# Reading rearranged columns back one slot later, and a second tile for the modulation's weights

## The chip, the cores and the metric

The kernel runs on one core of one Trainium2 chip. The metric is the device time of one execution in microseconds; the time of a kernel is the median over several executions.

## The reference

One row of 4096 tokens with 640 features goes through two networks, each behind a layer norm that is scaled and shifted by a modulation computed from `c`:

```python
mod = (_silu(c) @ w_mod).reshape(c.shape[0], 6, 1, -1)
sa, ca, ga, sb, cb, gb = (mod[:, 0], mod[:, 1], mod[:, 2], mod[:, 3], mod[:, 4], mod[:, 5])
h = _layernorm(x, axis=-1) * (1 + ca) + sa
x = x + ga * _A_ref(h, A_w1, A_b1, A_w2, A_b2)
h = _layernorm(x, axis=-1) * (1 + cb) + sb
x = x + gb * _B_ref(h, B_w_gate, B_w_up, B_w_down)
```

`_A_ref` is the first network: a real Fourier transform along the tokens, a two-layer complex MLP on each frequency (4 blocks of 160 features, relu between the layers, soft shrinkage with 0.01 behind them), and the inverse transform. `_B_ref` is the second network: `(silu(x @ w_gate) * (x @ w_up)) @ w_down` with 1728 hidden features. All data is float32.

## The kernel before

Matmuls run on float32r operands, each float32 operand split into a high and a low part, so that most products are three matmuls. The program has three stretches: layer norm and the first step of the Fourier transform; the first network's loop; the second network. The change lies in the loop.

The loop runs over 32 slots `p`, four to each of 8 chunks of frequencies (`ch = p // 4`, `b = p % 4`). Every engine executes its instructions in the order written here, and so does the queue of SP, which issues nearly all DMAs (`nc.sync.dma_start`): a DMA that waits holds all that is written behind it. In one slot PE does the following, in this order:

- `stage_l1` (lines 636 and 649): the first MLP layer of block `b`, from the chunk's tiles `z` (features 0 to 127 of a block) and `rz` (the narrow columns, features 128 to 159 of every block). Its third output goes to a PSUM bank that line 654 (`u`, on DVE, behind line 653 on ACT) evacuates.
- `stage_b` (line 552): the second Fourier step of the next chunk, from `g` and `tb`; twice where `b == 1`, once of them for the narrow columns.
- `stage_l2` (line 682): the second layer of the slot before, its results added into `tt` by DVE.
- `stage_i` (lines 735 to 737): the inverse step of a chunk seven slots back, in two halves, into `co`, which POOL's queue stores.

The narrow columns of the next chunk come out of `stage_b` in an order that `stage_l1` cannot use. They are rearranged through DRAM: `rem_high` (ACT, line 602) and `rem_low` (DVE, line 606) fill `rt`; `rem_move` stores `rt` into `rzd` (line 615) and reads it back in four DMAs into `rz` (line 618). All three are called in the slot with `b == 1`; `rz` is used first in the next slot with `b == 0`. Tile `rz` has two buffers.

The modulation is summed beside this: `mod_load(m, k)` loads 128 rows of one of its parts, 128 x 640, into `wm` (line 488, SP), and `mod_add(m, k)` (lines 493 and 495, DVE) multiplies it by a column of `sc` and adds it to `acc`. There are 20 such steps, five for each of four parts, and the tile `wm` has one buffer. The slots are written down in two tables, `mods` and `sums`; the list for a slot is called at the slot's end. For part `i` step `k`, the load is in slot 4 + 6i + k and the add in slot 5 + 6i + k, where it is followed by the load of the next step. So a load waits for the add written directly ahead of it, and has until the end of the next slot to land.

Other DMAs on SP in the loop: `move_x` in slots with `b == 0` (line 698, eight moves of `tt` into `xx`), `load_g` and `load_tb` in slots with `b == 3`, `load_e` in slot 26, and the loads of rows for the second network's start (`load_first_rows`, line 798) in slots 24 and 27 and behind the loop. Each slot's DMAs are issued in this order: `rem_move`, `move_x`, `load_g`, the slot's `mods`, `load_first_rows`.

The memory for a tile comes from pools. `low_p` holds `rt` and a tile `spare` that nothing uses; `p2` holds `wm`, `acc`, `xx` and others.

Of the kernel before, what the change touches and what calls it, by code (L numbers as in the profile page):

```python
# [6 lines left out]
F32 = mybir.dt.float32  # L7
# [6 lines left out]
P = 128  # L14
D = 640
# [6 lines left out]
NCH = 8  # L22
# [149 lines left out]
def body(tc, x, w1, b1, w2, b2, wg, wu, wd, c, wm, k_fa, k_tb, k_tx, k_bm, k_bx, k_ga, k_ge, k_id, out, dbg=None):  # L172
# [4 lines left out]
    def f32(ap):  # L177
        return ap.bitcast(F32)
# [21 lines left out]
    from contextlib import ExitStack  # L200
    with ExitStack() as top:
        low_p = top.enter_context(tc.tile_pool(name="low_p", bufs=1, reuse_waits="tile"))
        low_p.tile([P, 2552], F32, name="spare")
        per = top.enter_context(tc.tile_pool(name="per", bufs=1))
        ps = top.enter_context(tc.tile_pool(name="ps", bufs=2, space=PSUM))

# [30 lines left out]
        with ExitStack() as af:  # L237
# [47 lines left out]
            def weights_low(w, h, l, v, sg):  # L285
                dve.scalar_tensor_tensor(w[:, :, l], v, sg, f32(w[:, :, h]), op0=OP.mult, op1=OP.subtract)
# [182 lines left out]
            p2 = af.enter_context(tc.tile_pool(name="p2", bufs=1, side="right", reuse_waits="tile"))  # L469
# [14 lines left out]
            wmts = {}  # L484

            def mod_load(m, k):
                wmts[m, k] = p2.tile([P, D], F32, tag="wm", bufs=1, name=f"wm{m}_{k}")
                nc.sync.dma_start(wmts[m, k], wm[:, m, k, :])

            def mod_add(m, k):  # L490
# [37 lines left out]
            mods = {26: [(load_e,)]}  # L528
            sums = {}
            for i, m in enumerate((0, 2, 3, 4)):  # L530
                for k in range(5):
                    mods.setdefault(4 + 6 * i + k, []).append((mod_load, m, k))
                    mods.setdefault(5 + 6 * i + k, []).append((mod_add, m, k))
                sums.setdefault(11 + 6 * i if m < 4 else LAST, []).append((mod_sum, m, 1))
                if m == 2:
                    sums.setdefault(10 + 6 * i, []).append((mod_sum, m, 0))
# [7 lines left out]
            def width(ch):  # L544
                return 258 if ch == CE else 256

            def stage_b(ch, t):
                g, tb = gs[ch], tbs[ch]
                pb = bank0(1 if t == 4 else 0, [P, 2, 256], f"pb{ch}_{t}")
                col = slice(128 * t, 128 * t + 128)  # L550
                for j in range(4):
                    mm(pb[:, :, 64 * j:64 * j + 64], g[:, j, col], tb[:, j, :], start=True, stop=True)
                pbs[ch, t] = pb

            def evac_b(ch, t):
                pb = pbs[ch, t]
                z = lp.tile([P, 2, 2, 258], F32R, tag="z", bufs=4, name=f"z{ch}_{t}")
                zs[ch, t] = z
                act.activation(z[:, 0, :, 0:256], pb, AF.Identity, scale=ca1[:, t:t + 1])
                dve.scalar_tensor_tensor(z[:, 1, :, 0:256], pb, ca1[:, t:t + 1],  # L560
                                         f32(z[:, 0, :, 0:256]), op0=OP.mult, op1=OP.subtract)
                if ch == CE:
                    pool.tensor_copy(z[:, 0, :, 0:257:256], f32(edge[:, 0, t]))
                    pool.tensor_copy(z[:, 1, :, 0:257:256], f32(edge[:, 1, t]))
                    pool.tensor_copy(z[:, :, :, 257], zero[:, 0, 0])
# [8 lines left out]
            def evac_rh(ch, b):  # L574
                pb = pbs[ch, 4]
                if b == 0:
                    rzs[ch] = hp.tile([P, NB, 258], F32R, tag="rz", bufs=2, name=f"rz{ch}")
                    if ch == CE:
                        pool.tensor_copy(rzs[ch][:, :, 257], zero.rearrange("p a b c d -> p (a b c d)")[:, 0:4])
                q = slice(32 * b, 32 * b + 32)  # L580
                for i in range(2):
                    act.activation(rzs[ch][32 * i:32 * i + 32, b, 0:256], pb[q, i, :], AF.Identity,
                                   scale=ca1[q, 4:5])

            def evac_rl(ch, b):
                pb = pbs[ch, 4]
                r = rzs[ch]
                q = slice(32 * b, 32 * b + 32)
                for i in range(2):
                    rh = slice(32 * i, 32 * i + 32)  # L590
                    rl = slice(64 + 32 * i, 96 + 32 * i)
                    dve.scalar_tensor_tensor(r[rl, b, 0:256], pb[q, i, :], ca1[q, 4:5],
                                             f32(r[rh, b, 0:256]), op0=OP.mult, op1=OP.subtract)
                    if ch == CE:
                        pool.tensor_copy(r[rh, b, 0:257:256], f32(edge[q, 0, 4, i]))
                        pool.tensor_copy(r[rl, b, 0:257:256], f32(edge[q, 1, 4, i]))
# [3 lines left out]
            def rem_high(ch):  # L600
                rt = rts[ch] = low_p.tile([P, 2, 2, 258], F32R, tag="rt", name=f"rt{ch}")
                act.activation(rt[:, 0, :, 0:256], pbs[ch, 4], AF.Identity, scale=ca1[:, 4:5])

            def rem_low(ch):
                rt = rts[ch]
                dve.scalar_tensor_tensor(rt[:, 1, :, 0:256], pbs[ch, 4], ca1[:, 4:5], f32(rt[:, 0, :, 0:256]),
                                         op0=OP.mult, op1=OP.subtract)
                if ch == CE:
                    for hl in range(2):
                        pool.tensor_copy(rt[:, hl, :, 0:257:256], f32(edge[:, hl, 4]))  # L610
                    pool.tensor_copy(rt[:, :, :, 257], zero[:, 0, 0])

            def rem_move(ch):
                NN = width(ch)
                nc.sync.dma_start(rzd[ch, :, :, 0:NN], f32(rts[ch].rearrange("p l i k -> p (l i) k")[:, :, 0:NN]))
                r = rzs[ch] = hp.tile([P, NB, 258], F32R, tag="rz", bufs=2, name=f"rz{ch}")
                for q in range(4):
                    nc.sync.dma_start(f32(r[32 * q:32 * q + 32, :, 0:NN]),
                                      rzd[ch].rearrange("(b e) q k -> q e b k", b=NB)[q, :, :, 0:NN])
# [183 lines left out]
            for p in range(LAST + 1):  # L803
                ch, b = p // 4, p % 4
                on(shrink, p - 6)
                on(stage_l1, p)

                if b == 0:
                    todo = [(ch, 3)]
                else:  # L810
                    todo = [(ch + 1, 4)] * (b == 1) + [(ch + 1, b - 1)]
                todo = [q for q in todo if q[0] < NCH]
                for q in todo:
                    stage_b(*q)
                    if q[1] < 4:
                        evac_b(*q)
                for f, *a in sums.get(p, ()):
                    f(*a)

                if p == 0:  # L820
                    evac_rh(0, 3)
                if b == 1 and ch + 1 < NCH:
                    rem_high(ch + 1)
                on(tail_l1, p)
                on(shrink_high, p - 6)
                if p == 0:
                    evac_rl(0, 3)
                if b == 1 and ch + 1 < NCH:
                    rem_low(ch + 1)
                    rem_move(ch + 1)  # L830
                on(stage_l2, p - 1)
                on(stage_i, p - 7)
                on(shrink_low, p - 6)
                if p < LAST:
                    on(shrink_parts, p - 5)
                if b == 0 and ch:
                    for i in range(4):
                        move_x(ch - 1, i)
                if p == 0:
                    for job in prep2[3:]:  # L840
                        weights_low(*job)
                if b == 3 and 2 < ch + 2 < NCH:
                    load_g(ch + 2)
                    load_tb(ch + 2)
                for f, *a in mods.get(p, ()):
                    f(*a)
                if p == LAST - 4:
                    cf += [rp.tile([P, 2, D], F32, tag=tag, name=f"cf{tag}") for tag in ("rm", "rr")]
                    load_first_rows(rb + 16, rl, nc.sync)
                elif p == LAST - 1:  # L850
                    load_first_rows(0, rb - 16, nc.sync)
# [107 lines left out]
        with ExitStack() as ff:  # L959
# [15 lines left out]
            for n, (k, p) in enumerate(WG):  # L975
                STG.append(("w", n))
                if k == "g" and p:
# [22 lines left out]
            bufs = {"R": 2, "h1": 1, "wb": 2, "wt": 2, "wd": 1, "wdh": 2, "wdl": 2, "pc": 4, "px": 2, "gt": 2, "ho": 2,  # L1000
                    "h32": 1, "sg": 4, "s": 5, "gx": 2, "rb0": 1, "rb1": 1, "ra0": 1, "ra1": 1}
# [1008 lines left out]
            mv, rs, _ = fst[3]  # L2010
# [25 lines left out]
            for t in range(NS):  # L2036
                for n in range(NW):
                    if sum_at(n) == t:
                        a, b = sum_w(n)
# [69 lines left out]
```

## Time and profile before

| | us |
|---|---|
| median of 3 runs | 1487.83 |
| lowest and highest | 1484.5, 1488.16 |
| the profiled execution | 1483.82 |
| its span | 1482.0 |
| loop of the first network, from about 60 to 312 of the span | 252 |
| second network, 312 to the end | 1170 |

The profile is that of one execution; its times are microseconds from the start of the span. A row of the timeline has the start, the duration, the engine, the line, what is written and read and how many instructions are merged in the row; in brackets stands the idle time ahead of it and what ended that. SPq is the queue of SP. The granted clock is that of the tensor engine as a share of full speed. The ends of pipelined matmuls are modelled, so spacings are taken from their starts.

### The profile page before, as it was taken

The numbers are of one execution on the slowest core, as the hardware profiler recorded it, in microseconds if no ns is written. First come the engines' busy times: TensorE is split into PE (matmuls) and PEld (weight loads), VectorE is DVE, ScalarE is ACT, GpSimd is POOL, SyncE is SP. The second block draws the span as 40 slices with busy tenths as digits, with TensorE's granted clock in tenths as the row PEclk, the third lists the DMA queues.
The fourth block names the chain that finished last, engine by engine and source line by source line (L and its number), as shares of the span: only waits on it lengthen the run. The fifth ranks groups of instructions, "written<-read, shape, count | busy, mean of one in ns | idle before, by whom it ended". The sixth has DMA issues, their size and how long they took to land.

```text
span 1482.0 us, 23780 instructions
## 1 busy us (share of the span) xinstructions
PE 1432.4 (97%) x8736; PEld 1356.8 (92%) x8736; DVE 1023.8 (69%) x1841; ACT 759.9 (51%) x1470; POOL 411.6 (28%) x528
## 2 busy tenths in 40 slices
PE   6999999898999999999999999999999999999999
PEld 2799999876888888899999999999999999999999
DVE  8567777678787787757877756878656555465653
ACT  7657888645444555445545535554443334344331
POOL 5400100034563443313433323433211121111111
PEclk9999999999999999999999999999999999999999
DMA  9966767738767977696677797566774345944422
GB/s 378 328 207 197 230 206 226 218 95 280 272 228 251 363 258 242 213 398 229 208 235 242 263 350 255 200 233 228 291 287 151 120 156 179 349 154 139 146 75 83
DMA packets 162405, 339.41 MB, mean 229 GB/s; under 512 B 20656, under 2 KB 85872, under 8 KB 160240
## 3 DMA queue, kind: packets, MB, share of 16 engines
q1 hardware_dynamic: 153776, 320.35, 63.5%
q0 software_dynamic: 6928, 14.91, 3.3%
q10 hardware_dynamic: 1584, 2.62, 0.5%
q8 instruction: 69, 1.13, 0.3%
q14 instruction: 48, 0.39, 0.1%
HBM read 238.35 MB, written 90.31 MB: 222 GB/s over the span
## 4 chain that ended last, share of the span: by engine, by line
PE 68%; DMA 10%; issue 10%; DVE 6%; POOL 3%; ACT 3%; SPq 1%; POOLq 0%; DVEq 0%; ACTq 0%
PE pd L1984 21%; PE pw L1790 7%; PE pw L1792 7%; PE pw L1791 7%; DMA wt<-td 4%; PE pg L1713 3%; PE pg L1714 3%; PE pg L1715 3%; PE pw L1801 2%; PE pw L1803 2%; PE pw L1802 2%; PE pc L682 2%; PE pl L636 2%; PE py L1443 2%; DMA hs<-ho 1%
## 5 line engine op out<-in xcount | busy, mean ns | idle before, releaser
L1984 PE MATMUL pd<-wdh,a 128*128 128x320 f32 x1672 | 382.4, 310 | 2.8 <-DVE a L1750 2.0
L1984 PEld LDWEIGHTS pd<-wdh,a 128*128 128x128 f32 x1672 | 282.9, 188 | 4.0 <-DVE a L1750 2.6
L1984 PE MATMUL pd<-wdl,a 128*128 128x320 f32 x868 | 267.3, 309 | 0.0
L1956 DVE TENSOR_TENSOR x<-x,pd 128x320 f32<-128x320 f32 x384 | 178.9, 482 | 100.7 <-PE pd L1984 93.2
L1246 DVE TENSOR_TENSOR wb<-r,wb 128x512 fp32r<-128x512 f32 (+3 forms) x172 | 162.8, 954 | 18.8 <-ACT wb L1243 17.4
L1984 PEld LDWEIGHTS pd<-wdl,a 128*128 128x128 f32 x868 | 163.1, 188 | 0.4
L1790 PE MATMUL pw<-h,wt 128*128 128x384 f32 x416 | 141.0, 339 | 6.4 <-DMA wt<-td 5.0
L1792 PE MATMUL pw<-h,wt 128*128 128x384 f32 x416 | 139.2, 335 | 0.0
L1791 PE MATMUL pw<-h,wt 128*128 128x384 f32 x416 | 139.2, 335 | 0.0
L1337 ACT ACTIVATE wdh<-wdr 128x640 fp32r<-128x640 f32 x84 | 60.6, 734 | 152.4 <-PE pd L1984 144.1
L1243 ACT ACTIVATE wb<-r 128x512 fp32r<-128x512 f32 (+3 forms) x172 | 117.9, 704 | 29.4 <-PE pw L1803 21.0
L1834 POOL TENSOR_TENSOR sg<-s_x,sg 128x384 f32<-128x384 f32 x24 | 25.1, 1048 | 351.7 <-DVE s_x L1816 351.7
L1792 PE MATMUL pw<-h,wb 128*128 128x384 f32 x312 | 104.7, 336 | 0.7 <-DVE wb L1246 0.7
L1790 PE MATMUL pw<-h,wb 128*128 128x384 f32 x312 | 105.0, 337 | 0.0
L1791 PE MATMUL pw<-h,wb 128*128 128x384 f32 x312 | 104.7, 335 | 0.0
L1715 PE MATMUL pg<-ht,wb 128*128 128x512 f32 x260 | 101.7, 391 | 2.2 <-DVE wb L1246 2.2
L1713 PE MATMUL pg<-ht,wb 128*128 128x512 f32 x260 | 102.3, 393 | 1.2 <-ACT wb L1243 1.2
L1714 PE MATMUL pg<-ht,wb 128*128 128x512 f32 x260 | 101.5, 390 | 0.0
L1341 DVE TENSOR_TENSOR wdl<-wdr,wdh 128x640 fp32r<-128x640 f32 x84 | 75.7, 910 | 33.6 <-ACT wdh L1337 33.4
L1837 DVE TENSOR_TENSOR a<-sg,a 128x384 fp32r<-128x384 f32 x104 | 71.9, 700 | 31.7 <-ACT a L1836 31.2
L1790 PEld LDWEIGHTS pw<-h,wt 128*128 128x128 f32 x416 | 78.1, 188 | 9.9 <-DMA wt<-td 4.1
L1791 PEld LDWEIGHTS pw<-h,wt 128*128 128x128 f32 x416 | 78.2, 188 | 0.0
(264 smaller groups left out, 3315.6 us busy)
## 6 DMA issues: line engine op xcount, KB each, us to landing
wt<-td SPq DMA_DIRECT2D x104, 512.0 KB, 5.2
hs<-ho SPq DMA_DIRECT2D x52, 512.0 KB, 5.4
h<-hs SPq DMA_DIRECT2D x32, 768.0 KB, 8.0
r<-in_B_w_gate_dram SPq DMA_DIRECT2D x36, 640.0 KB, 4.4
r<-in_B_w_up_dram SPq DMA_DIRECT2D x36, 640.0 KB, 4.8
wdr<-wdd SPq DMA_DIRECT2D x35, 640.0 KB, 4.5
td<-wt SPq DMA_DIRECT2D x25, 512.0 KB, 4.9
g<-s SPq DMA_DIRECT2D x28, 320.0 KB, 5.5
```

The lines of the kernel that those rows point to most:

```text
L1243: act.activation(wbs[t, n][:, 0, ks, e], raw[t, n][:, ks, e], AF.Copy)
L1246: dve.tensor_tensor(wbs[t, n][:, 1, ks, e], raw[t, n][:, ks, e], f32(wbs[t, n][:, 0, ks, e]), op=OP.subtract)
L1341: dve.tensor_tensor(l[:, f], wdraw[t, p][:, f], f32(h[:, f]), op=OP.subtract)
L1713: mm(b, wh, hh, start=(kk == 0), stop=False)
L1714: mm(b, wh, hl, start=False, stop=False)
L1715: mm(b, wl, hh, start=False, stop=(kk == 4))
L1790: mm(b, w(0, kp), a[:, kp, 0], start=start and kp == 0, stop=False, skip_group_check=not start)
L1791: mm(b, w(0, kp), a[:, kp, 1], start=False, stop=False, skip_group_check=not start)
L1792: mm(b, w(1, kp), a[:, kp, 0], start=False, stop=kp == 1, skip_group_check=not start)
L1837: Step("V", cv_ + 0.1, lambda: dve.tensor_tensor(o[:, 1], sg, f32(o[:, 0]), op=OP.subtract), (("ah", key),), ("act", t, fc, a), free=("sg" ...
L1956: dve.tensor_tensor(x2[:, e], x2[:, e], x[0][:, :320], op=OP.add)
L1984: mm(pd[g, hf][0][:, :320], l, m, start=i == 0, stop=i == len(s) - 1 and not (last and len(gs) > 1))
```

## The change

`rem_move` is cut in two: it keeps the store to `rzd`, and the allocation of `rz` and the four reads become `rem_read`, called in the slot with `b == 2`, ahead of that slot's `mods`. The tile of a modulation load is taken in turn from `p2` and from `low_p`, each with one buffer, so that there are two; `spare` shrinks by the 640 elements that the second takes. Every load stands one slot earlier in the table (3 + 6i + k), its add where it was.

```diff
-        low_p.tile([P, 2552], F32, name="spare")
+        low_p.tile([P, 1912], F32, name="spare")
...
             def mod_load(m, k):
-                wmts[m, k] = p2.tile([P, D], F32, tag="wm", bufs=1, name=f"wm{m}_{k}")
+                wmts[m, k] = (p2, low_p)[len(wmts) % 2].tile([P, D], F32, tag="wm", bufs=1, name=f"wm{m}_{k}")
                 nc.sync.dma_start(wmts[m, k], wm[:, m, k, :])
...
                 for k in range(5):
-                    mods.setdefault(4 + 6 * i + k, []).append((mod_load, m, k))
+                    mods.setdefault(3 + 6 * i + k, []).append((mod_load, m, k))
                     mods.setdefault(5 + 6 * i + k, []).append((mod_add, m, k))
...
             def rem_move(ch):
                 NN = width(ch)
                 nc.sync.dma_start(rzd[ch, :, :, 0:NN], f32(rts[ch].rearrange("p l i k -> p (l i) k")[:, :, 0:NN]))
+
+            def rem_read(ch):
+                NN = width(ch)
                 r = rzs[ch] = hp.tile([P, NB, 258], F32R, tag="rz", bufs=2, name=f"rz{ch}")
                 for q in range(4):
                     nc.sync.dma_start(f32(r[32 * q:32 * q + 32, :, 0:NN]),
...
                 if b == 1 and ch + 1 < NCH:
                     rem_low(ch + 1)
                     rem_move(ch + 1)
+                if b == 2 and ch + 1 < NCH:
+                    rem_read(ch + 1)
                 on(stage_l2, p - 1)
```

## The prediction

> **What bounds the kernel now.** I read the page first, then the busy time of each engine in the three stretches of the program, then the waits of the first network's stretch, and then its timeline on SP, DVE and PE.
>
> ```profile
> span 1482.0 us, 23780 instructions
> ...
> PE 1432.4 (97%) x8736; PEld 1356.8 (92%) x8736; DVE 1023.8 (69%) x1841; ACT 759.9 (51%) x1470; POOL 411.6 (28%) x528
> ...
> 60.00:312.00 252.00, 238.98 (x1810) 235.23 (x1809) 182.69 (x342) 179.48 (x374) 26.54 (x51) 0.98 0.68 211
> 312.00:1482.00 1170.00, 1145.56 (x6761) 1096.48 (x6759) 795.60 (x1363) 536.72 (x1023) 355.95 (x410) 1.00 0.66 226
> ```
>
> The two window rows give stretch and length, then busy time of PE, PEld, DVE, ACT and POOL, the granted clock, the DMA share and GB/s. PE bounds the whole program. The change touches only the stretch from 60 to 312, the slotted loop of the first network: there PE is busy for 239 of 252 us, at a mean clock of 0.98 instead of 1.00. Some 13 us of idle time and a little clock are all that can be won there. The waits say which idle time the change can reach.
>
> ```profile
> SPq L618 <- DMA rzd<-rt: 31.6, 7, 7.0
> ...
> DVE acc L495 <- DMA wm<-in_w_mod_dram: 13.5, 5, 6.7
> ...
> PE pi L735 <- DVE u L654: 6.8, 2, 4.9
> ```
>
> Read from the top: who waited for whom, us in total, times, longest. SP's queue stands seven times, once for each rearranged chunk, until the narrow columns have landed in DRAM (rzd); only then may line 618 read them back. DVE stands five times for a weight tile wm of the modulation. PE stands twice for `u`, an evacuation that DVE makes. The timeline shows that these are one chain; first SP's queue (start, duration, line, transfer, count):
>
> ```profile
> 110.70 0.57 SPq L615 DMA_DIRECT2D rzd<-rt  x1
> 114.89 1.74 SPq L618 DMA_DIRECT2D rz<-rzd  x4
> 116.74 5.83 SPq L488 DMA_DIRECT2D wm<-in_w_mod_dram  x2
> ...
> 255.47 0.54 SPq L488 DMA_DIRECT2D wm<-in_w_mod_dram  x1
> ...
> 257.62 0.59 SPq L615 DMA_DIRECT2D rzd<-rt  x1
> 265.29 1.79 SPq L618 DMA_DIRECT2D rz<-rzd  x4
> 267.18 0.38 SPq L488 DMA_DIRECT2D wm<-in_w_mod_dram  x1
> ```
>
> The wm loads at 116.74 and 267.18 are those of slots 5 and 25 (b = 1). They were free to go earlier, but they stand in the queue behind the four reads of rz, and those behind the landing of rzd. DVE and ACT at the same two places:
>
> ```profile
> 112.21 0.55 DVE L493 TENSOR_SCALAR acc<-wm,sc 128x640 f32<-128x640 f32 x1 [0.34 <-DMA wm<-in_w_mod_dram]
> ...
> 116.50 0.81 DVE L724 TENSOR_TENSOR xl<-xx,xh 128x640 fp32r<-128x640 f32 x1
> ...
> 118.70 0.38 ACT L653 ACTIVATE u<-pl 64x256 f32<-64x256 f32 x1
> ...
> 121.31 0.88 DVE L495 SCALAR_TENSOR_TENSOR acc<-wm,sc,acc 128x640 f32<-128x640 f32 x1 [3.99 <-DMA wm<-in_w_mod_dram]
> ...
> 123.51 0.47 DVE L654 SCALAR_TENSOR_TENSOR u<-pl,b1r,u 64x256 f32<-64x256 f32 x1
> ...
> 259.61 0.89 DVE L495 SCALAR_TENSOR_TENSOR acc<-wm,sc,acc 128x640 f32<-128x640 f32 x1 [0.19 <-DMA wm<-in_w_mod_dram]
> ...
> 264.24 0.82 DVE L724 TENSOR_TENSOR xl<-xx,xh 128x640 fp32r<-128x640 f32 x1
> ...
> 267.07 0.38 ACT L653 ACTIVATE u<-pl 64x256 f32<-64x256 f32 x1
> ...
> 271.74 0.89 DVE L495 SCALAR_TENSOR_TENSOR acc<-wm,sc,acc 128x640 f32<-128x640 f32 x1 [6.68 <-DMA wm<-in_w_mod_dram]
> ```
>
> The adds of slots 6 and 26 stand 3.99 and 6.68 us for those loads; the other three of the five waits are 13.5 - 10.7 = 2.8 us together. DVE works in order, so the evacuation of `u` (line 654) stands behind each add, and PE needs the PSUM bank that `u` frees. PE at both places and, between them, at a place where nothing waits:
>
> ```profile
> 121.79 0.30 PE L737 MATMUL pi<-xh,bm 128*128 128x320 f32 x1
> ...
> 124.04 0.49 PE L735 MATMUL pi<-xh,bm 128*128 128x320 f32 x1 [1.95 <-DVE u L654]
> ...
> 127.77 0.40 PE L636 MATMUL pl<-rz,w1c 128*128 128x256 f32 x2
> ...
> 262.67 0.31 PE L737 MATMUL pi<-xh,bm 128*128 128x320 f32 x1
> ...
> 263.96 0.40 PE L636 MATMUL pl<-rz,w1c 128*128 128x256 f32 x2
> ...
> 264.91 0.40 PE L636 MATMUL pl<-rz,w1c 128*128 128x256 f32 x2
> ...
> 269.30 0.30 PE L737 MATMUL pi<-xh,bm 128*128 128x320 f32 x1
> ...
> 274.46 0.64 PE L735 MATMUL pi<-xh,bm 128*128 128x320 f32 x1 [4.87 <-DVE u L654]
> ...
> 278.17 0.40 PE L636 MATMUL pl<-rz,w1c 128*128 128x256 f32 x2
> ```
>
> **The change, part by part.** *What the two stalls cost.* From the last matmul of line 737 ahead of the gap to the second rz run of line 636 behind it, the same work takes 264.91 - 262.67 = 2.24 us undisturbed, 127.77 - 121.79 = 5.98 us at the first stall and 278.17 - 269.30 = 8.87 us at the second. The excess is 3.74 + 6.63 = 10.37 us. Of it 1.95 + 4.87 = 6.82 us are gaps; the rest, 1.79 and 1.76 us, is slow work after the gaps:
>
> ```profile
> 117.00:128.00 11.00, 9.05 (x58) 8.80 (x57) 6.95 (x13) 6.70 (x15) 0.62 (x1) 0.84 0.61 177
> ```
>
> The granted clock around the first stall is 0.84, so even a gap of 1.95 us cost clock. Beside this row stands a rule of the Trainium skill, "TensorE: Matmul & The Clock Gate", section "HAM oscillation": only idle gaps of more than about 3.4 us re-throttle the clock. By that rule the first stall would be worth its gap alone, and the sum 10.37 - 1.79 = 8.58 us. Here the trace disagrees with it, and I take the measured 10.37.
>
> *Do both stalls go?* The add of slot 6 takes its tile from a load in slot 4 instead of 5, the add of slot 26 from slot 24 instead of 25; neither has a read-back ahead of it any more. The load that goes out at 255.47, in slot 24 behind the moves of the tt columns, has landed by 259.61 (the add there waited 0.19 us for it); in the changed kernel that place holds the tile of slot 26, which DVE wants at 264.24 + 0.82 = 265.06, so 5 us are spare. At 112.21 the tile of slot 4's place has landed likewise, and it is wanted at 116.50 + 0.81 = 117.31.
>
> *What is late next?* From add to `u` DVE needs 123.51 - 121.31 = 2.20 us. Started at 117.31, `u` begins at 119.51 (ACT's part of it is done at 118.70 + 0.38 = 119.08) and ends at 119.98; PE wants the bank at about 121.79 + 0.15 = 121.94, the spacing of these matmuls being about half of the 0.30 that one lasts. At the second place ACT is done at 267.45, `u` at 267.92, and PE wants it at 269.45. Margins 2.0 and 1.5 us: PE runs on.
>
> *The read-back, one slot later.* On SP its four DMAs move past the wm load of slot b = 1 and nothing else; POOL's queue is not touched. It still waits for the landing of rzd, which decided before. The load that now precedes it, in slot 5, waits for the add at 112.21, which ends at 112.76, 2.1 us ahead of 114.89; in slot 25 for the add at 259.61, which ends at 260.50, 4.8 us ahead of 265.29. So the read-back leaves when it left before. What it needs:
>
> ```profile
> L618 SPq DMA_DIRECT2D rz<-rzd x28: 309/424/1514, 94.0 to 266.6; - x28
> ...
> DMA to landing us min/median/max: 2.5/2.8/3.7
> ...
> 116.45 0.40 PE L636 MATMUL pl<-rz,w1c 128*128 128x256 f32 x2
> ...
> 257.36 0.40 PE L636 MATMUL pl<-rz,w1c 128*128 128x256 f32 x2
> ```
>
> One slot is 263.96 - 257.36 = 6.60 us of PE. Without the second stall PE asks for the last chunk's rz at 263.96 + 6.60 = 270.56; the last read starts at 266.6 and lands 2.8 to 3.7 us later, at 269.4 to 270.3. That margin is 0.3 to 1.2 us, the tightest of the change: the stall that goes was also cover for this read. Chunk 2, read at 114.89, asks at 116.45 + 6.60 = 123.05 and has it by 114.89 + 1.74 + 3.7 = 120.3: 2.7 us. Against the last chunk speaks a rule of the Trainium skill, "DMA: Bandwidth & Descriptors", section "Queues, rings and completion order": on each DMA engine descriptors are consumed in ring order, so the wm load that now stands ahead is served before the read. No run here shows that order yet.
>
> *Costs at nothing.* 28 reads and 20 loads stay 28 and 20, no compute instruction is added, and the second tile lies in memory that was spare. A load still waits in its slot for an add of the same slot, as before, so what stands behind it on SP (rzd, load_g, the tt moves) is held no longer than now. Two slots are 13.2 us for a transfer for which this took at most:
>
> ```profile
> L488 SPq DMA_DIRECT2D wm<-in_w_mod_dram x20: 328/365/1392, 108.7 to 272.6; - x20
> ...
> DMA to landing us min/median/max: 3.0/4.2/5.7
> ```
>
> *Does the gain reach the end?* In the chain that ended last, at the seam of the two networks, stands the load of the first network's last rows, which the next matmuls wait for:
>
> ```profile
> 311.99 2.95 DMA cfrr<-s
> ```
>
> It follows the last store of the first network, the loads of the second stand behind it on SP, and all of them move up together. The second network is PE at 1145.56 of 1170 us and is unchanged; I take its change as 0, with 3 us to either side, since the three runs of this kernel spread over 3.7 us (1484.5 to 1488.16).
>
> The sum: 10.37 us less at most 0.4 for a read that is just late, 10.2 taken. The profiled execution took 1483.82 us (span 1482.0), so it would be 1473.6. The median of the runs is 4.0 us above the profiled one; the same 10.2 from 1487.83 give 1477.6.
>
> **The rivals.** *The read-back becomes the late one.* If the wm load of slot 25 does delay it, by up to the 1.5 us that lie between landings of 4.2 and 5.7, the last chunk starts about 1.2 us late, and after such a gap the slow clock takes up to 1.8 more: 10.4 - 3 = 7.4 us gained, 1480.4. For it speaks the margin of 0.3 us; against it that the load has 4.8 us of lead and lands in 4.2.
>
> *The second network gives it back.* Its own waits for DMAs could swallow the lead; nothing says so, since it depends on the first in a chain, but should 7 us or more of the 10.2 go, the time is 1484.6 to 1487.8, no change.
>
> *The change does not do what it says.* An add still waits, say because the load two slots ahead is held by the tt moves on SP. One of two stalls left gives 1481.2 (the first gone alone, 1484.1).
>
> *Slower.* The load in slot b = 1 waits for an add and holds the read-back behind it in every chunk; PE then starts each chunk late. Place: the first rz matmul of chunks 2 to 7. It decides once the add ends later than rzd lands (2.1 us of margin in slot 5, 4.8 in slot 25) and by more than the read's own margin (2.7 in chunk 2). To end 4.5 us above the present time it must cost 10.4 + 4.5 = 14.9 us, 2.5 in each of six chunks: the add of slot 5 would have to end 7.3 us later than it does (2.1 + 2.7 + 2.5), while the change takes waits out of DVE. With it the time is about 1493.
>
> **How the numbers follow.** About 0.3% of the time, 4.5 us, is what a measurement of this kernel can tell from no change. Forecast as summed 0.72; read-back late 0.11; one stall left 0.06, half of it still faster by 0.3%; given back 0.07; slower 0.04. That makes faster 0.86, same 0.10, slower 0.04. The range runs from 1477.6 less 3 for the second network and 2 for the runs' level, 1472.6, up to the late read with 3 us given back, 1483.4.
>
> **What would show it.** Right: in the changed profile the adds of line 495 no longer wait longer than 1 us, the wm load of slot 25 stands ahead of the rz reads on SP, the two gaps of line 735 are gone, the mean clock of the stretch is above 0.98, and the stretch is 10 us shorter. Wrong: a new gap ahead of the rz matmuls of line 636 at the start of the last chunk, an add that still waits, or a length from the loop's end to the span's end that has grown instead.

## The result, and the profile after

| | before | after |
|---|---|---|
| median of 5 runs, us | 1485.26 | 1475.6 |
| lowest to highest, us | 1484.5 to 1488.16 | 1473.78 to 1480.82 |
| profiled execution (span), us | 1483.82 (1482.0) | 1477.1 (1475.3) |

The ratio of after to before is 0.9934, with a 95% interval of 0.9911 to 0.9957: 9.7 us less by the medians, 6.4 to 13.2 us by the interval. In a second comparison (the run named e10 below, six runs) it is 0.9951, 0.9938 to 0.9964, or 7.3 us. The change makes the kernel faster, by 0.5 to 0.7%.

The page of after, and then its busy time in the two stretches, from the windows view (columns as in the prediction; the boundary is moved by 7 us):

```profile
span 1475.3 us, 23779 instructions
...
PE 1431.8 (97%) x8736; PEld 1358.4 (92%) x8736; DVE 1026.0 (70%) x1841; ACT 759.5 (51%) x1470; POOL 409.8 (28%) x528
```

```profile
60.00:305.00 245.00, 237.91 (x1813) 233.99 (x1812) 184.66 (x344) 179.23 (x375) 26.46 (x52) 0.99 0.71 218
305.00:1475.00 1170.00, 1146.24 (x6758) 1099.33 (x6758) 795.78 (x1361) 536.57 (x1022) 354.68 (x410) 1.00 0.66 226
```

That the second stretch keeps its 1170 us follows from where I put the boundary. Counted by the work, from the first matmul of slot 0 to the first of `first_y`, the step behind the loop, there are 233.3 us instead of 241.4, 8.1 less. From there to the end are 1170.4 us instead of 1169.5, and slot 0 starts 0.4 us later; together these are the 6.7 us of the span. The clock of the loop's stretch rose from 0.98 to 0.99. SP's queue, DVE and PE at the two places (timeline of after; from line 616 on its lines stand three to five further down: 618 is 621, 636 is 639, 737 is 740):

```profile
110.83 0.57 SPq L615 DMA_DIRECT2D rzd<-rt  x1
112.47 0.33 SPq L488 DMA_DIRECT2D wm<-in_w_mod_dram  x1
115.24 1.75 SPq L621 DMA_DIRECT2D rz<-rzd  x4
118.12 0.35 SPq L488 DMA_DIRECT2D wm<-in_w_mod_dram  x1
...
253.63 0.59 SPq L615 DMA_DIRECT2D rzd<-rt  x1
256.77 0.34 SPq L488 DMA_DIRECT2D wm<-in_w_mod_dram  x1
261.53 1.78 SPq L621 DMA_DIRECT2D rz<-rzd  x4
263.41 1.32 SPq L522 DMA_DIRECT2D et<-in_k_ge_dram  x1
```

The wm load of slots 5 and 25 now goes out between the store of rzd and the read of rz, in time that SP spent waiting. Grouped by line, the adds of the loop:

```profile
L495 DVE SCALAR_TENSOR_TENSOR acc<-wm,sc,acc 128x640 f32<-128x640 f32 x16 | 14.0, 877 | 0.0
```

The last number is DVE's idle time ahead of them: 0.0, where it was 13.5 us. And PE at both places:

```profile
121.92 0.30 PE L740 MATMUL pi<-xh,bm 128*128 128x320 f32 x1
122.06 0.31 PE L738 MATMUL pi<-xh,bm 128*128 128x320 f32 x1
...
124.16 0.39 PE L639 MATMUL pl<-rz,w1c 128*128 128x256 f32 x2
...
265.66 0.30 PE L740 MATMUL pi<-xh,bm 128*128 128x320 f32 x1
...
267.90 0.40 PE L639 MATMUL pl<-rz,w1c 128*128 128x256 f32 x2
```

From 121.92 to 124.16 are 2.24 us, the undisturbed figure of the prediction, where there were 5.98. From 265.66 to 267.90 are 2.24 us as well, where there were 8.87.

### The profile page after: what moved, and what is told of

Same layout as the page of the kernel before. It is cut to its first block, busy times and chain, and to the rows that moved or that the text cites. A ratio compares the mean times of both kernels' runs of the same rounds, so it can differ in the third digit from the quotient of the medians.

```text
span 1475.3 us, 23779 instructions
## 1 busy us (share of the span) xinstructions
PE 1431.8 (97%) x8736; PEld 1358.4 (92%) x8736; DVE 1026.0 (70%) x1841; ACT 759.5 (51%) x1470; POOL 409.8 (28%) x528
## 4 chain that ended last, share of the span: by engine, by line
PE 50%; DMA 3%; DVE 1%; ACT 1%; issue 0%; POOL 0%; SPq 0%
PE pd L1989 19%; PE pw L1795 7%; PE pw L1797 7%; PE pw L1796 7%; DMA wt<-td 3%; PE pw L1806 2%; PE pw L1808 2%; PE pw L1807 2%; PE pr L1909 1%; PE py L1448 1%; PE pt L1512 1%; PE pd L1999 0%; DVE wdl L1346 0%; DVE ho L1553 0%; ACT h L1516 0%
```

## The experiments

Each is compared with the kernel before on the same chip. For the loop I give the length of slots 7 and 8 and of slots 27 and 28 in the profile of each run, counted from the first matmul of `stage_l1` of a slot to that of the next; the two stalls of before lie in them.

| run | slots 7 + 8 | slots 27 + 28 | all four | ratio to before, 95% interval |
|---|---|---|---|---|
| before | 16.97 | 22.40 | 39.37 | |
| after | 13.21 | 15.77 | 28.98 | 0.9934, 0.9911 to 0.9957 |
| e1, read-back alone | 13.22 | 22.97 | 36.19 | 0.9978, 0.9964 to 0.9993 |
| e2, tiles and early loads alone | 13.22 | 15.76 | 28.98 | 0.9935, 0.9915 to 0.9956 |
| e6, e1 with late load_e | 13.22 | 15.80 | 29.02 | 0.9933, 0.9909 to 0.9957 |
| e8, second tile alone | 15.67 | 22.71 | 38.38 | 0.9995, 0.9981 to 1.0009 |
| e5, after with read-back at b = 3 | 14.55 | 22.32 | 36.87 | 0.9971, 0.9956 to 0.9987 |
| e3, after with a third tt | 13.21 | 16.15 | 29.36 | 0.9936, 0.9913 to 0.9959 |
| e7, after with chunk 1 direct | 13.22 | 15.90 | 29.12 | 0.9930, 0.9904 to 0.9955 |
| e9, e3 and e7 | 13.22 | 15.86 | 29.08 | 0.9925, 0.9906 to 0.9945 |
| e10, after again | 13.22 | 16.64 | 29.86 | 0.9951, 0.9938 to 0.9964 |
| e4, before with adds on POOL | 13.22 | 28.24 | 41.46 | 1.0112, 1.0088 to 1.0136 |

**e1: the read-back move alone.** Before, with `rem_move` cut in two; tiles and loads as before.

```diff
+                if b == 2 and ch + 1 < NCH:
+                    rem_read(ch + 1)
```

> Only the read-back moves to the slot with b = 2; one wm tile, loads where they were. Theory A (what stalls PE is the wm load standing behind the read-back on SP): the load of slot 5 goes out when the add of its slot ends, at about 112.8, lands 3.0 to 5.7 us later, at 115.8 to 118.5, and is wanted at 117.3; the add waits at most 1.2 us, less than the 2 us that PE can spare. Both gaps of line 735 go, the loop is 10.4 us shorter than before, the time about 9 to 10 us less: as much as the whole change. Theory B (the second tile and the extra slot are what counts; the load still starts only after the add ahead of it): the waits shrink but stay over 2 us at one of the two places, and the gain is under 5 us.

Measured 1484.09 against 1486.23 us. Slots 7, 8 and 27 are as theory A has them (6.63, 6.59 and 6.63 us): both gaps of line 735 are gone. But the gain is that of theory B, because a third add became late (timeline of e1, SP, then DVE and PE):

```profile
260.88 1.98 SPq L621 DMA_DIRECT2D rz<-rzd  x4
262.96 1.67 SPq L522 DMA_DIRECT2D et<-in_k_ge_dram  x1
264.74 0.37 SPq L488 DMA_DIRECT2D wm<-in_w_mod_dram  x1
...
272.31 0.88 DVE L495 SCALAR_TENSOR_TENSOR acc<-wm,sc,acc 128x640 f32<-128x640 f32 x1 [5.24 <-DMA wm<-in_w_mod_dram]
...
273.34 2.27 PE L510 MATMUL pm<-ones,acc 128*128 128x1 f32 x10 [4.00 <-DVE acc L495]
```

The last wm load, of slot 26, now stands behind the read-back and behind `load_e` (1280 KB). In the kernel before, the stall of slot 27 had hidden that. The wait moved from the add of slot 26 to that of slot 27. The DMA engines served the load last as well: the packets of `load_e` start between 265.28 and 269.65, those of the wm load, issued 1.8 us behind it, between 269.13 and 270.97, and it lands 7.5 us after its issue (at most 5.7 in the kernel before).

**e2: the tiles and the early loads alone.** After, with the read-back in its old place.

```diff
                     rem_move(ch + 1)
-                if b == 2 and ch + 1 < NCH:
                     rem_read(ch + 1)
```

> Only the second wm tile and the loads one slot earlier; the read-back stays in the slot with b = 1, ahead of that slot's load. Theory A: the tile for the add of slot 6 is loaded in slot 4 and that of slot 26 in slot 24, ahead of the read-back, so both gaps go as well: 9 to 10 us less than before, each half of the change being enough by itself. Theory C (the place of the read-back is what counts): the load behind it still holds SP, and the gain is under 5 us.

Measured 1477.9 against 1486.23 us, the ratio of the whole change. In slot 25 SP still reads back first (263.20) and loads wm behind it (265.09), but that tile is wanted only in slot 27, and its add at 269.35 waited 0.37 us. This half carries the change; the read-back move adds nothing that these runs can tell.

**e6: e1 with load_e one slot later.** The last wm load is then ahead of it.

```diff
-            mods = {26: [(load_e,)]}
+            mods = {27: [(load_e,)]}
```

> The run with the read-back move alone, and load_e in slot 27 instead of 26, behind the last wm load. In that run both gaps of line 735 were gone, but the add of slot 27 waited 5.24 us (its load went out at 264.74, behind the read-back and load_e) and PE stood 4.00 us at line 510. Theory A2 (what stands ahead of the last load on SP and on the DMA engines decides): without load_e ahead it is issued at about 263 and lands at 267 to 268, the add waits about 1 us, the gap at line 510 goes, and the time is 6 to 7 us below that run, at the changed kernel's. Theory B2 (one tile is too few in any order): the add still waits over 3 us and the gain is under 3 us.

Measured 1478.67 against 1488.24 us, again the whole gain, with one wm tile. The adds of slots 25 to 27 waited 0.69, 0.46 and 0 us:

```profile
265.32 0.88 DVE L495 SCALAR_TENSOR_TENSOR acc<-wm,sc,acc 128x640 f32<-128x640 f32 x1 [0.46 <-DMA wm<-in_w_mod_dram]
...
270.80 0.88 DVE L495 SCALAR_TENSOR_TENSOR acc<-wm,sc,acc 128x640 f32<-128x640 f32 x1
```

So theory A2 holds: what stands ahead of a load decides, and e1 failed for `load_e` alone.

**e8: the second tile alone.** Before, with the tile from two pools in turn; loads and read-back where they were.

```diff
-                wmts[m, k] = p2.tile([P, D], F32, tag="wm", bufs=1, name=f"wm{m}_{k}")
+                wmts[m, k] = (p2, low_p)[len(wmts) % 2].tile([P, D], F32, tag="wm", bufs=1, name=f"wm{m}_{k}")
```

> The kernel before with the second wm tile alone: loads in their old slots, read-back in its old place. Theory A (order on SP decides, not the number of tiles): the loads of slots 5 and 25 still stand behind the read-back, the adds of slots 6 and 26 still wait about 4 and 6.7 us, the gaps of line 735 stay at 2 and 5 us, the time is that of before within 2 us. Theory B (the second tile is what counts, since a load no longer waits for the add ahead of it): gaps go, 9 us less.

Measured 1487.06 against 1488.24 us: no change. The add and PE at the two places, in the timeline of e8:

```profile
121.17 0.89 DVE L495 SCALAR_TENSOR_TENSOR acc<-wm,sc,acc 128x640 f32<-128x640 f32 x1 [4.29 <-DMA wm<-in_w_mod_dram]
...
123.90 0.41 PE L738 MATMUL pi<-xh,bm 128*128 128x320 f32 x1 [2.19 <-DVE u L657]
...
270.08 0.89 DVE L495 SCALAR_TENSOR_TENSOR acc<-wm,sc,acc 128x640 f32<-128x640 f32 x1 [6.74 <-DMA wm<-in_w_mod_dram]
...
272.81 0.64 PE L738 MATMUL pi<-xh,bm 128*128 128x320 f32 x1 [4.72 <-DVE u L657]
```

Waits of 4.29 and 6.74 us, gaps of 2.19 and 4.72: both stalls stand with two tiles. A second buffer is worth nothing until the load is written ahead of what blocks it.

**e4: the adds on POOL.** Before, with each step in two instructions on POOL (the first step of each part in one, which is not shown here).

```diff
-                    dve.scalar_tensor_tensor(acc, wmt, sc[:, k:k + 1], acc, op0=OP.mult, op1=OP.add)
+                    pool.tensor_scalar(wmt, wmt, sc[:, k:k + 1], None, op0=OP.mult)
+                    pool.tensor_tensor(acc, acc, wmt, op=OP.add)
```

> The kernel before, with the modulation's multiply and add on POOL (two instructions a step instead of one on DVE); the read-back and the loads stay as they were, so the tiles come as late as before. Theory A (PE stood because DVE, which frees its bank, stood in order behind the add): POOL now waits 4 and 7 us for the same two loads, the gaps of line 735 go, and the time is 8 to 10 us less than before; what it may cost is that the stores of co stand behind POOL's wait. Theory F (the late DMAs or the traffic slow PE in themselves): gaps of 2 and 5 us stay wherever the adds run.

Measured 1504.43 against 1486.23 us. Slots 7, 8 and 27 (6.63, 6.59, 6.62) have no gap although POOL waits for late tiles, which is theory A's point: PE stood because the add stood on DVE. The time that theory A gave, 8 to 10 us less, was missed by far: it is 18 us more by the medians. In the profile the loop takes 254.0 us instead of 241.4, and what follows it 8.1 us more than before, which nothing here explains. The price that was expected of the stores came elsewhere in the loop (waits of e4 between 100 and 310):

```profile
POOL wm L495 <- DMA wm<-in_w_mod_dram: 31.3, 12, 6.8
...
PE pm L511 <- POOL acc L496: 8.7, 1, 8.7
...
PE pm L506 <- POOL acc L496: 3.2, 1, 3.2
...
PE pb L553 <- DMA tb<-in_k_tb_dram: 3.4, 1, 3.4
```

The two POOL instructions take 1.89 and 1.55 us where DVE's one takes 0.88, tiles come free later, loads behind them on SP (`tb` among them) too, and PE's sums of `acc` stand for the last add.

**e5: the read-back later still.** After, ahead of `load_g` in the next slot.

```diff
-                if b == 2 and ch + 1 < NCH:
+                if b == 3 and ch + 1 < NCH:
                     rem_read(ch + 1)
```

> The changed kernel with the read-back one slot later still, in the slot with b = 3. In the changed kernel the last chunk's rz landed at 266.39 and PE wanted it at 266.94, 0.55 us of margin. Now its reads stand behind load_e (1280 KB) as well, which holds the 16 DMA engines for about 5 us. Theory G (the margin is as thin as that): a gap of 4 to 6 us ahead of the rz matmuls at the start of the last chunk, with 1.7 us of slow clock, and no gap at chunks 2 to 6, whose margins are 2.7 to 5 us; 5 to 8 us above the changed kernel. Theory H (DMAs have more room than that): no gap of more than 1 us, the time of the changed kernel within 2 us.

Measured 1484.28 against 1488.24 us: most of the gain is gone again, 4.0 us left of some 10. SP's queue and PE at the start of the last chunk:

```profile
258.59 0.55 SPq L522 DMA_DIRECT2D et<-in_k_ge_dram  x1
264.95 1.80 SPq L621 DMA_DIRECT2D rz<-rzd  x4
...
271.93 0.76 PE L639 MATMUL pl<-rz,w1c 128*128 128x256 f32 x2 [3.62 <-DMA rz<-rzd]
```

The gap of 3.62 us ahead of rz makes slot 28 15.70 us instead of 9.15: theory G, a little under its 4 us. Against it there is a second gap, 1.10 us at chunk 2, whose margin I had put at 2.7.

**e3 and e7: two losses seen in single profiles.** The profile of after has a wait that before has hardly, at the loop's end:

```profile
284.19 0.49 DVE L687 TENSOR_TENSOR tt<-pc,b2t 128x320 f32<-128x320 f32 x1 [1.94 <-PE pl L652]
...
293.79 0.41 PE L738 MATMUL pi<-xh,bm 128*128 128x320 f32 x1 [0.97 <-ACT xh L722]
...
295.27 0.64 PE L739 MATMUL pi<-xl,bm 128*128 128x320 f32 x1 [1.06 <-DVE xl L727]
```

The row names line 652, whose matmul ended at 283.82, but DVE waited for tile `tt`, whose last move out (issued at 278.28) completed at 284.02. e3 gives `tt` a third place, in `low_p`:

```diff
+                        n = len(tts) % 3
+                        tts[ch, q] = (p2, p2, low_p)[n].tile([P, 2, D], F32, tag="tt", bufs=(2, 2, 1)[n],
```

> The changed kernel with a third place for tile tt. In its profile DVE waited 1.94 us for a move of tt at 284.19, after which PE had gaps of 0.97 and 1.06 us and slow clock at the loop's end, 2.7 us in all. Theory D (that wait for the slowest part of the move is what made the loop's end longer): the wait goes, the two gaps go or shrink to the one of 1.03 us that the kernel before has, and the time is 1 to 3 us below the changed kernel. Theory E (the chain of the last shrink steps on ACT and DVE is the bound there): gaps stay, the time is that of the changed kernel within 1 us.

Measured 1478.62 against 1486.23 us, the ratio of after. Its profile has neither the wait nor the long gaps (0.51 us are left), but the profile of e2, with two places, has not either. The profile of e6, with two places, has it (1.53 us at 286.97, two gaps of 0.66 and 1.07 us behind it). So the wait belongs to single executions, and e3 cannot decide more. e7 takes chunk 1's narrow columns the way of chunk 0's:

```diff
-                if b == 1 and ch + 1 < NCH:
-                    rem_high(ch + 1)
+                if b == 1 and 0 < ch and ch + 1 < NCH:
+                    rem_high(ch + 1)
+                elif ch == 0 and b:
+                    for i in ((), (0,), (1,), (2, 3))[b]:
+                        evac_rh(1, i)
```

and `evac_rl` likewise in place of `rem_low`, `rem_move` and `rem_read`.

> The changed kernel, but the narrow columns of chunk 1 are arranged by ACT and DVE directly, as those of chunk 0 are, without the way through DRAM. In the profiles so far slot 4, where chunk 1 starts, took 5.96 to 9.55 us where 5.76 would do, because its rz landed at about 98. Theory I (that landing is a loss of its own, 0.2 to 3.8 us): slot 4 takes 5.8 us, the time is 1 to 3 us below the changed kernel. Theory J (the 8 extra instructions each on ACT and DVE, about 3.8 us each, in slots 1 to 3 delay PE as much): slots 1 to 3 grow by what slot 4 loses, no gain or a loss up to 2 us.

Measured 1477.75 against 1488.24 us, a ratio of 0.9930. Slot 4 took 6.39 us, not 5.8; no gain over after can be told. PE no longer waits there for `rz`; it waits 0.41 us at line 685 (at 100.01) for an add of DVE into `tt`.

**e9 and e10: both edits together, and the changed kernel again.**

> The changed kernel with the third place for tt and with chunk 1's narrow columns arranged directly. Neither alone moved the median by what a measurement can tell; their profiles showed 2.7 and 0.9 us less in the loop than the changed kernel's profile. Theory K (both were losses of one profiled execution, seldom in the median): the time is that of the changed kernel within 2 us. Theory L (they add up): 3 us below it.

> The changed kernel again, beside the run with both extra edits on the same chip, with a second profile. Theory K: in this profile DVE need not wait for a move of tt in slot 29, the loop's end is then as long as in the kernel before, the span is 9 to 11 us below 1482.0, and the ratio to before is 0.993 again. Theory L: the wait of 1.9 us and the two gaps at the loop's end are there again.

e9 took 1475.27 us, e10 1480.4, before 1487.72. The medians differ by 5 us, which favours theory L over K, but the intervals (0.9906 to 0.9945 and 0.9938 to 0.9964) overlap; e9 is the lowest ratio of the study, and that it beats the changed kernel is likely, not shown. The second profile of after, e10, shows which losses come and go:

```profile
140.24 0.49 DVE L687 TENSOR_TENSOR tt<-pc,b2t 128x320 f32<-128x320 f32 x1 [3.63 <-DMA xx<-tt]
...
144.36 0.41 PE L738 MATMUL pi<-xh,bm 128*128 128x320 f32 x1 [1.59 <-DVE u L657]
...
263.99 3.04 SPq L621 DMA_DIRECT2D rz<-rzd  x4
...
269.42 0.47 PE L639 MATMUL pl<-rz,w1c 128*128 128x256 f32 x2 [0.63 <-DMA rz<-rzd]
```

The wait for a move of `tt` is there, at the add of slot 9 this time (0.87 us at that add in before, 1.34 in after), and slot 10 takes 8.46 us instead of 6.61; the loop's end is clean; and the last chunk's rz is late by 0.63 us. The four reads took 3.04 us to issue, in after 1.78: the third alone took 1.70 us instead of 0.42. The span is 1474.6, 7.4 below before, not the 9 to 11 of theory K.

## Why the prediction was right, point by point

- *The sum of the two stalls, 10.37 us.* The four slots went from 39.37 to 28.98, that is 10.39 us. The same four slots explain three of the runs as well: -3.2 us in e1 (ratio times 1486 gives -3.3), -10.4 in e2 (-9.7), -1.0 in e8 (-0.7). They do less for e5 (-2.5, by the ratio -4.3, interval -1.9 to -6.5) and do not explain e4 (+2.1, by the ratio +16.6), which loses in other slots too. The 10.37 held a piece of luck: in e8 the same first stall cost 1.3 us less (15.67 against 16.97), where the clock stayed at 1.00.
- *The chain read-back, wm load, add, u, PE.* Shown link by link: e8 keeps the order on SP and keeps the stalls, e6 changes the order alone and loses them, e4 takes the add off DVE and the gaps of line 735 go although the tiles are late.
- *Nothing else is late next.* Right for the change as a whole. It would have been wrong for the read-back move alone, as my expectation of e1 was: I had followed the loads of slots 5 and 25 and not that of slot 26, behind `load_e`. The prediction credited "neither has a read-back ahead of it any more" to the whole change; by e2 it is the loads' earlier slots that do it, and the move is not needed for it.
- *The read-back leaves when it left before.* It left 4.41 and 7.90 us after the store of rzd, before 4.19 and 7.67.
- *Its margin at the last chunk, 0.3 to 1.2 us.* Measured: landed at 266.39, wanted at 266.94, 0.55 us. In e10 the margin was missed by 0.63 us, and slot 28 took 10.02 us instead of 9.15: a late read is real, at 0.9 us and not 3. But the cause that the rival gave, the wm load ahead of the read, is not what the traces show: its packets had ended at 261.54 in after and at 263.81 in e10, when SP issued the first read (261.53 and 263.99). In e10 the reads began 0.8 us later in the slot, and the third issued slowly. They began 8.31 us behind the store of rzd, before 7.67; whether the wm load held up the landing of that store by some tenths is open. The order on the DMA engines, which no run had shown when the prediction was made, is seen in e1. e5 shows how little room there is.
- *The chunk 2 margin, 2.7 us.* Too wide to judge by: one slot later on SP used all of it in e5.
- *What follows the loop, 0 with 3 us to either side.* The size held. In the profile of after 2.6 us came back at the loop's end (from the start of slot 31 to the first matmul of `first_y` 17.96 us, before 15.41) and 0.9 behind it, so that its span fell by 6.7 and not 10; in e10 1.85 came back in slot 10 and 0.9 in slot 28. The loop's end is that long in e6 too (17.71), and 14.8 to 15.6 us in the other ten profiles. Whether the changed kernel meets such waits more often than before is open.
- *The signs.* The adds wait 0.0 us, the wm load of slot 25 goes out ahead of the reads, both gaps are gone, and the clock is 0.99; the loop is 8.1 us shorter in after and 8.0 in e10, not 10. Two of the signs of being wrong appeared, each in one of the two profiles: from the start of slot 31 to the span's end after takes 1188.4 us, before 1184.9 (e10 1185.2), and e10 has the gap ahead of rz. Neither took back the gain.
- *The time.* 1477.6 forecast, 1475.6 and 1480.4 measured. The first lies 2 us below the forecast because the level moved: over five runs the median of before is 1485.26 and not 1487.83. For the profiled execution 1473.6 was forecast, and 1477.1 and 1476.34 were measured. The forecast gain of 10.2 lies inside the first interval and 1 us above the second: the loop gave what the sum said, and 0 to 3 us of it were lost again in single executions.

## What to carry to other kernels

When an engine waits for a load, look at what the load's queue was doing: if it stood for another transfer's landing, the order of the queue is the fault, and one more buffer (e8) does nothing until the load is written ahead of the wait. When a stall goes, go through every later load of the same kind, since the stall was cover for them: here the next one stood behind 1280 KB and took 7 of the 10 us back (e1). Issue a read-back early rather than late; with all waits gone it is the next thing that PE stands for (e5).

## What the runs showed of the hardware that was not expected

- **One sixteenth of a transfer lands late beside a load of instructions.** The last move of `tt` in the profile of after reports its landing in 16 parts; 15 of them came between 281.37 and 282.33, the last at 284.02. At 281.70 a 16 KB packet of the instruction queue (q8) occupied a DMA engine for 0.96 us. In e10 such a packet of 1.23 us stands at 135.13, and the last part of a move landed at 140.16, the others by 137.58; in e6 one of 0.95 us at 284.34, the last part at 286.79, the others by 285.02. Slow issues on SP stand beside such packets too: in after, e10 and e3 a packet (at 263.33, 264.76 and 263.15) falls on a DMA that SP was issuing (`et`, the third and the second read of `rz`), and that issue took 1.32, 1.70 and 1.20 us instead of about 0.4. In e10 this met the read with the thinnest margin. That the packet is the cause is a reading of the times and was not tried.
- **The same gap costs clock in one execution and not in another.** The granted clock of the same window, before (gap of 1.95 us, 0.84) and in e8 (gap of 2.19 us):

```profile
117.00:128.00 11.00, 8.81 (x70) 8.55 (x69) 6.77 (x12) 6.46 (x15) 0.62 (x1) 1.00 0.84 286
```

  Here it stayed at 1.00, and slots 7 and 8 lost 2.5 us in all instead of 3.8. In e2 a gap of 2.07 us in slot 4 brought the window from 96 to 106 to 0.83. In the profile of after two gaps of 0.97 and 1.06 us close together brought the window from 290 to 300 to 0.83; a single gap of 1.03 us at the loop's end of before left that from 300 to 310 at 1.00. The rule of 3.4 us in the Trainium skill, "TensorE: Matmul & The Clock Gate", section "HAM oscillation", does not fit: gaps of about 2 us were enough, though not each time. Of the 1.8 us of slow work that the prediction counted for the first stall, e8 had 0.3: the rest was a matter of that execution.
